# Values of the first attention jobs loaded into the accumulator, and four first-layer tiles accumulated ahead, two to a PSUM bank

## The chip, the cores and the metric

The kernel runs on one core of a Trainium2 chip. The metric is device microseconds (us) of one execution; lower is better. A core has a matmul engine (PE, with its weight loads shown as PEld), a vector engine (DVE), a scalar engine (ACT), a general engine (POOL) and a queue engine (SP) from which this kernel issues all its transfers (DMAs). Each engine works through its own list of instructions in a fixed order and waits at the first one whose inputs are not ready.

## The reference

Inputs are q, k, v of 2 batches x 8 heads x 576 positions x 64, and the weights of two feed-forward layers. For every batch and head two attentions are added: one of q, k, v averaged over groups of 4 positions (each output row is repeated 4 times), and one local attention in which a position sees only positions less than 4 away:

```
q_d, k_d, v_d = means over groups of 4 positions
out_up    = repeat(softmax(q_d k_d^T / 8) v_d, 4)
out_local = softmax(where(|i - j| < 4, q k^T / 8, -1e9)) v
x = (out_up + out_local) as 1152 tokens x 512
h = x @ w_in (512 x 2048);  x = (h * sigmoid(h)) @ w_out (2048 x 512)
out = sum over 4 experts e of p[e] * (relu(x @ w1[e]) @ w2[e])      (512 x 1024 x 512)
```

Everything is 32-bit floating point; the large products are made of three matmuls each, from a rounded value and its rest (h and l: h*h, h*l, l*h).

## The kernel before, in words

**Attention.** The work is cut into 16 jobs: 2 batches x 2 ranges of positions (256 and 320, c = 0 and 1) x 4 pairs of heads. Jobs 0 to 3 are the first range of the first batch. For a job of the first range SP loads one tile with k and q (`load_kq`, L244, 419 KB), the values in groups of four for the averaged attention (`load_vg`, L257, 288 KB) and the values in windows for the local one (`load_vw`, L250, 144 KB). A job of the second range has its own kq (323 KB) and vw tiles (L252) and reuses the averaged values of its pair of heads. The tile `vg` has one buffer, which the tail queries `qt` (L262, the last 64 positions of a batch) use too; `vw` and each kind of `kq` have two buffers. POOL folds `vg` into the averaged values `vd` (L265), and from job 4 on also q and k of a job into their averages (`qbd`, `kd`). Jobs 0 to 3 do the latter on PE and DVE (`pool_kq_first`, L292, L300).

A job then goes: scores on PE (L328, L334), maximum and subtraction on DVE (L341, L342), exponential on ACT (L346); averaged scores on PE (L352), their maximum on DVE (L366, L367) and exponential on ACT (L368); sums and division on DVE (L349 to L377) and ACT (L378); transposes on PE (L388, L390), copied by ACT (L391, L398); products with the values on PE (L416, L420); the sum of both attentions (L423, L425), and its split into `xh` (ACT, L432) and `xl` (DVE, L433). The output bank of L416 and L420 has one buffer, so a job's values wait for the split of the job before.

**First feed-forward layer.** Its weights come as 32 pieces of 512 KB (units 0 to 7 of four pieces each) through three staging buffers (L164). A piece is decoded on ACT (L189, L190), DVE (L191, L195), ACT (L197) and POOL (L198). The decoding of unit 1 is put behind job 2's `xl` on DVE, that of units 2 and 3 behind job 3's. The next load waits for a staging buffer. `g1_step` makes one 128-wide tile of h for a chunk of tokens (12 matmuls, L495), `g1_evac` turns it into g on ACT (L514 tanh, L520) and DVE (L515, L521). `g2_step` makes the second product and adds it up in `acc`, a tile of 128 x 4608 floats that is first written there. For the first chunk (256 tokens, jobs 0 to 3) the first `HOLD` = 3 tiles of h are accumulated ahead: as soon as job hp is split, `start_mm(hp)` adds its 3 matmuls to each of them. The tiles of h and g2 share three PSUM banks (`mm`); the three held tiles take them all, one bank each.

**Order.** Every step gets a priority (`at_tick`, `prio`): a load of job 1's `vg`, for example, has -26, the third weight piece -27, the kq of jobs 4 and 5 -21 and -18. A scheduler that simulates a timeline puts each engine's list in order by readiness in its simulation and then by priority. `follow` and `after` add an order edge between two instructions without a semaphore wait. The lists are made once, before the run.

**Experts** (from about 300 us on): PE products (L495, L699) with DVE, ACT and POOL work beside them; outputs are stored at the end.

Of the kernel before, what the change touches and what calls it, by code (L numbers as in the profile page):

```python
# [9 lines left out]
F32 = mybir.dt.float32  # L10
# [11 lines left out]
HP = NH // 2  # L22
# [18 lines left out]

SPLIT_AT = (-14, -11, -8, -6, -4, -4, -4, -4, -1, -1)
LOAD_AT = (-27, -13, -10)
HOLD = 3
LEAD_LOAD = 23
LEAD_SPLIT = 8
LEAD_ATTN = 11
# [14 lines left out]
def attention_moe_kernel(ctx, tc, kqa, kqb, qtl, va, vb, w64, w1d, w2d, dpr, out):  # L62
    nc = tc.nc
    PE, ACT, DVE, POOL, SP = nc.tensor, nc.scalar, nc.vector, nc.gpsimd, nc.sync
# [25 lines left out]
    acc = const.tile([128, 9 * 512], F32, name="acc")  # L90
# [31 lines left out]
    def follow(i, earlier, reason):  # L122
        tc.add_manual_dep(i.ins, earlier.ins.name, mybir.DependencyInfo(mybir.DependencyClass.NoSync, mybir.DependencyReason.DATA),
                          reason=reason)
# [81 lines left out]
    ac = actx.enter_context(tc.tile_pool(name="ac", bufs=1))  # L206
# [29 lines left out]
        pass  # L236

    kd, vd, atd = {}, {}, {}
    qt_t = {}

    def load_kq(j):
        kw = S + 6 if j.c == 0 else CT[1] + 6
        j.kq = a2.tile([128, kw + j.n], F32, tag=f"kq{j.c}", name="kq")
        SP.dma_start(out=j.kq, in_=(kqa, kqb)[j.c][j.b, j.hp])  # L244
        j.k, j.q = j.kq[:, :kw], j.kq[:, kw:]

    def load_vw(j):
        j.vw = a2.tile([72, 640], F32, tag="vw", name="vw")
        if j.c == 0:
            SP.dma_start(out=j.vw[:, 0:512], in_=va[j.b, j.hp, :, 1024:1536])  # L250
        else:
            SP.dma_start(out=j.vw, in_=vb[j.b, j.hp])  # L252

    def load_vg(j):
        if j.c == 0:
            j.vg = ac.tile([128, 256, 4], F32, tag="vg", name="vg")[0:72]
            SP.dma_start(out=j.vg, in_=va[j.b, j.hp, :, 0:1024])  # L257

    def load_tail(l):
        t = ac.tile([128, 256, 4], F32, tag="vg", name="qt")  # L260
        l.t = t[:, 0:64]
        SP.dma_start(out=l.t, in_=qtl[l.b].rearrange('p (n r) -> p n r', r=4))  # L262

    def padd(o, a, b):
        POOL.tensor_tensor(out=o, in0=a, in1=b, op=ALU.add)  # L265
# [51 lines left out]
    def after(i, earlier):  # L317
        follow(i, earlier, "PSUM bank")
# [125 lines left out]
    def plan_jobs():  # L444
        k = 0
        for b in range(NB):
            for c in range(2):
                for hp in range(HP):
                    j = Job()
                    j.i = k  # L450
                    j.b, j.c, j.hp, j.n, j.nb = b, c, hp, CT[c], CB[c]
                    t = FIRST + PER * k
                    if k > 1:
                        at_tick(t - 4, 9, load_kq, j)
                    else:
                        at_tick(FIRST - 9, k, load_kq, j)
                    at_tick(t, 9, load_vg, j)
                    at_tick(t + 1, 9, load_vw, j)
                    at_tick(t, 5, local_scores, j)
                    at_tick(t, 6, local_max, j)  # L460
                    at_tick(t, 7, pool_kq if k > 3 else pool_kq_first, j)
                    at_tick(t + 1, 4, local_exp, j)
                    at_tick(t + 2, 4, down_scores, j)
                    at_tick(t + 2, 5, down_max, j)
                    at_tick(t + 2, 6, local_sum, j)
                    at_tick(t + 3, 3, norm, j)
                    at_tick(t + 3, 8, pool_v, j)
                    at_tick(t + 5, 2, trans, j)
                    at_tick(t + 6, 1, values, j)
                    at_tick(t + 7, 0, split_x, j)  # L470
                    k += 1
            l = Job()
            l.b, l.nb = b, 0
            t = FIRST + PER * (8 * b + 4)
            at_tick(t, 9, load_tail, l)
            at_tick(t + 2, 8, tail_pool, l)
            at_tick(t + 4, 5, tail_scores, l)
# [15 lines left out]
    def mm3(ps, pairs, first, last):  # L493
        n = len(pairs)
        ins = [PE.matmul(out=ps, lhsT=l, rhs=r, start=(first and i == 0), stop=(last and i == n - 1))  # L495
               for i, (l, r) in enumerate(pairs)]
        return ins[0], ins[-1]

    def g1_pairs(u0, ft, k, c):
        wh, wl = unit[u0 + ft // 4]  # L500
        s = slice(k * 512 + (ft % 4) * 128, k * 512 + (ft % 4) * 128 + 128)
        return [(wh[:, s], xh[:, k, c]), (wh[:, s], xl[:, k, c]), (wl[:, s], xh[:, k, c])]
# [8 lines left out]
    def g1_evac(ps, ft, n):  # L511
        th = tmp_p[0].tile([128, tmp_p[1]], F32, tag="th", name="th")
        gf = tmp_p[0].tile([128, tmp_p[1]], F32, tag="gf", name="gf")
        ACT.activation(out=th[:, 0:n], in_=ps[:, 0:n], func=ACTF.Tanh, scale=0.5)  # L514
        DVE.scalar_tensor_tensor(out=gf[:, 0:n], in0=th[:, 0:n], scalar=1.0, in1=ps[:, 0:n],  # L515
                                 op0=ALU.add, op1=ALU.mult)
        flush()

        def fin():
            latest[ACT] = ACT.activation(out=gh[ft][:, 0:n], in_=gf[:, 0:n], func=ACTF.Copy)  # L520
            latest[DVE] = DVE.tensor_tensor(out=gl[ft][:, 0:n], in0=gf[:, 0:n], in1=gh[ft][:, 0:n].bitcast(F32), op=ALU.subtract)  # L521

        pend.append(fin)

    def mm_tile():
        return mm_p.tile([128, 512], F32, tag="mm", name="mm")
# [239 lines left out]
    hold = []  # L766

    def start_mm(hp):
        for i in range(HOLD):
            if hp == 0:  # L770
                hold.append(mm_tile())
            mm3(hold[i][:, 0:256], g1_pairs(0, i, hp, slice(0, 256)), hp == 0, hp == HP - 1)

    main_parts.append(start_mm)
    plan_jobs()
    for hp in range(HP):
        at_tick(FIRST + PER * hp + 8, 9, start_mm, hp)
# [31 lines left out]
    def next_step(n=1):  # L809
        prio(step[0])  # L810
        step[0] += n

    for hf in range(2):
        u0 = 4 * hf
        dt = 48 / (12 * len(CHUNKS[hf]))
        for ci, (o, n) in enumerate(CHUNKS[hf]):
            lastc = ci == len(CHUNKS[hf]) - 1
            for ft in range(8):
                next_step(dt)
                if hf == 0 and ci == 0 and ft < HOLD:  # L820
                    g1_evac(hold[ft], ft, 256)
# [138 lines left out]
```

## Time and profile before

| | |
|---|---|
| times of 3 runs | 689.97, 691.39, 691.98 us, median 691.39 us |
| profiled execution | span 693.6 us; no other time of it was recorded |
| PE busy | 659.5 us, 95% of the span |
| PEld busy | 641.9 us, 93% |
| DVE busy | 440.3 us, 63% |
| ACT busy | 332.0 us, 48% |
| POOL busy | 247.5 us, 36% |
| mean granted PE clock | 0.974 |

The span runs from the first to the last instruction of the profiled execution. "Busy" is an average over stages with different limits, so the stage of a change has to be looked at by itself. The granted clock is 1.00 at 2.4 GHz and 0.50 at 1.2 GHz.

### The profile page before, as it was taken

The page shows a single profiled execution, that of the slowest core. Times are in us where ns is not written, and L with a number is a line of the kernel's source. Part 1 is how long each engine was busy: PE and PEld are TensorE (multiplying, and loading weights), DVE is VectorE, ACT ScalarE, POOL GpSimd, SP SyncE. Part 2 cuts the span into 40 slices and gives each one's busy share as a digit, 9 for nine tenths or more (in the row PEclk, how much of TensorE's full clock was granted, in tenths as well). Part 3 has the DMA queues.
Part 4 walks back from the last instruction along what each step waited for, and adds up shares of the span by engine and source line. Part 5 has one row for each costly group of instructions (what it writes and reads, how often), then busy time and mean ns, then how long its engine had stood idle before and what let it go on. Part 6 is the DMA issues. An engine that isn't in the chain of part 4 may idle for free.

```text
span 693.6 us, 13797 instructions
## 1 busy us (share of the span) xinstructions
PE 659.5 (95%) x5516; PEld 641.9 (93%) x5516; DVE 440.3 (63%) x882; ACT 332.0 (48%) x753; POOL 247.5 (36%) x346
## 2 busy tenths in 40 slices
PE   4779779999999999999999999999999999999996
PEld 3659669999999999999999999999999999999996
DVE  4678967638664643675665985548855669756444
ACT  4559766647653532544335643345533356433321
POOL 4344762114240000344264432456232654322210
PEclk9597989999999999999999999999999999999999
DMA  8665663105250210042001420004300010000001
GB/s 248 215 183 166 184 176 96 34 1 161 92 174 1 81 44 1 1 144 70 1 1 48 136 61 1 1 2 122 93 31 1 1 60 3 1 32 17 17 31 45
DMA packets 16927, 48.16 MB, mean 69 GB/s; under 512 B 2976, under 2 KB 4256, under 8 KB 16864
## 3 DMA queue, kind: packets, MB, share of 16 engines
q1 hardware_dynamic: 16864, 47.29, 22.0%
q8 instruction: 43, 0.70, 0.4%
q14 instruction: 20, 0.16, 0.1%
HBM read 44.93 MB, written 2.36 MB: 68 GB/s over the span
## 4 chain that ended last, share of the span: by engine, by line
PE 83%; DMA 6%; DVE 6%; ACT 2%; issue 2%; POOL 1%; SPq 0%; ACTq 0%; DVEq 0%; POOLq 0%
PE mm L495 53%; PE p L699 26%; DMA stg<-in_w_dram 3%; DMA vg<-in_va_dram 2%; DVE dec L191 1%; DVE dec L195 1%; DVE gl L521 1%; PE s L328 1%; PE o L420 1%; PE t L388 1%; PE o L416 1%; DVE acc L727 1%; DVE gf L515 0%; POOL vg L265 0%; PE s L352 0%
## 5 line engine op out<-in xcount | busy, mean ns | idle before, releaser
L495 PE MATMUL mm<-xh,wbuf 128*128 128x256 f32 (+2 forms) x1280 | 268.7, 296 | 3.4 <-ACT xh L432 2.6
L495 PEld LDWEIGHTS mm<-xh,wbuf 128*128 128x128 f32 x1280 | 211.0, 190 | 4.7 <-ACT xh L432 3.0
L495 PE MATMUL mm<-xl,wbuf 128*128 128x256 f32 (+2 forms) x640 | 189.8, 297 | 0.0
L681 POOL TENSOR_TENSOR r<-r 128x128 f32<-128x128 f32 x160 | 93.5, 597 | 183.2 <-ACT r L675 143.7
L684 DVE TENSOR_TENSOR h<-r,h 128x384 fp32r<-128x384 f32 (+1 forms) x128 | 91.4, 717 | 64.6 <-ACT h L683 64.4
L495 PEld LDWEIGHTS mm<-xl,wbuf 128*128 128x128 f32 x640 | 121.6, 190 | 0.1
L683 ACT ACTIVATE h<-r 128x384 fp32r<-128x384 f32 (+1 forms) x128 | 73.2, 577 | 85.3 <-POOL r L681 54.1
L495 PE MATMUL mm<-gh,wbuf 128*128 128x256 f32 (+2 forms) x512 | 106.0, 300 | 6.4 <-ACT wbuf L197 3.5
L699 PE MATMUL p<-wext,h 128*128 128x256 f32 x672 | 91.5, 279 | 0.0
L495 PEld LDWEIGHTS mm<-gh,wbuf 128*128 128x128 f32 x512 | 83.8, 191 | 8.0 <-ACT wbuf L197 3.7
L699 PE MATMUL p<-wbuf,h 128*128 128x256 f32 x672 | 84.5, 278 | 0.0
L699 PEld LDWEIGHTS p<-wext,h 128*128 128x128 f32 x672 | 84.4, 188 | 0.0
L699 PEld LDWEIGHTS p<-wbuf,h 128*128 128x128 f32 x672 | 81.2, 188 | 0.0
L495 PE MATMUL mm<-gl,wbuf 128*128 128x256 f32 (+2 forms) x256 | 74.7, 296 | 0.5 <-DVE gl L521 0.5
L675 ACT ACTIVATE r<-mm 128x512 f32<-128x512 f32 x48 | 28.7, 597 | 75.5 <-PE mm L495 75.1
L681 DVE TENSOR_TENSOR r<-r 128x128 f32<-128x128 f32 x96 | 33.5, 349 | 37.7 <-ACT r L675 33.0
L495 PEld LDWEIGHTS mm<-gl,wbuf 128*128 128x128 f32 x256 | 48.6, 190 | 0.8 <-DVE gl L521 0.8
L521 DVE TENSOR_TENSOR gl<-gf,gh 128x256 fp32r<-128x256 f32 (+2 forms) x64 | 34.8, 547 | 18.0 <-ACT gh L520 15.4
L198 POOL TENSOR_TENSOR wbuf<-dec,wbuf 128x512 fp32r<-128x512 f32 x24 | 32.5, 1360 | 31.1 <-ACT wbuf L197 20.2
L727 DVE SCALAR_TENSOR_TENSOR acc<-p,pr,acc 128x256 f32<-128x256 f32 (+1 forms) x63 | 36.1, 605 | 5.9 <-PE p L699 5.9
L626 POOL TENSOR_TENSOR wext<-kst,wext 128x512 fp32r<-128x512 f32 x8 | 10.7, 1344 | 78.4 <-ACT wext L624 42.9
L515 DVE SCALAR_TENSOR_TENSOR gf<-th,mm 128x256 f32<-128x256 f32 (+2 forms) x64 | 28.4, 449 | 15.3 <-ACT th L514 13.6
(122 smaller groups left out, 980.2 us busy)
## 6 DMA issues: line engine op xcount, KB each, us to landing
stg<-in_w_dram SPq DMA_DIRECT2D x32, 512.0 KB, 4.3
kst<-in_w2d_dram SPq DMA_DIRECT2D x16, 512.0 KB, 3.6
kst<-in_w1d_dram SPq DMA_DIRECT2D x12, 512.0 KB, 3.6
kq<-in_kqa_dram SPq DMA_DIRECT2D x8, 419.0 KB, 3.3
kq<-in_kqb_dram SPq DMA_DIRECT2D x8, 323.0 KB, 10.8
vg<-in_va_dram SPq DMA_DIRECT2D x8, 288.0 KB
stg<-in_w1d_dram SPq DMA_DIRECT2D x4, 512.0 KB
vw<-in_vb_dram SPq DMA_DIRECT2D x8, 180.0 KB
```

The lines of the kernel that those rows point to most:

```text
L191: i = DVE.scalar_tensor_tensor(out=ai, in0=ai, scalar=3, in1=v[:, :, 0], op0=ALU.logical_shift_left, op1=ALU.bitwise_or)
L198: POOL.tensor_tensor(out=l[:, c], in0=a, in1=h[:, c].bitcast(F32), op=ALU.subtract)
L495: ins = [PE.matmul(out=ps, lhsT=l, rhs=r, start=(first and i == 0), stop=(last and i == n - 1)) for i, (l, r) in enumerate(pairs)]
L515: DVE.scalar_tensor_tensor(out=gf[:, 0:n], in0=th[:, 0:n], scalar=1.0, in1=ps[:, 0:n], op0=ALU.add, op1=ALU.mult)
L521: latest[DVE] = DVE.tensor_tensor(out=gl[ft][:, 0:n], in0=gf[:, 0:n], in1=gh[ft][:, 0:n].bitcast(F32), op=ALU.subtract)
L626: b = eng.tensor_tensor(out=l[:, r], in0=x, in1=h[:, r].bitcast(F32), op=ALU.subtract)
L675: ACT.activation(out=r[:, 0:4].rearrange("p s t -> p (s t)"), in_=ps[:, 0:512], func=ACTF.Relu)
L681: latest[eng] = eng.tensor_tensor(out=r[:, o], in0=r[:, a], in1=r[:, b], op=op)
L683: ACT.activation(out=h, in_=r[:, part], func=ACTF.Copy)
L684: latest[DVE] = DVE.tensor_tensor(out=l, in0=r[:, part], in1=h.bitcast(F32), op=ALU.subtract)
L699: ins = [PE.matmul(out=ps, lhsT=x, rhs=y, start=(opens and k == 0 and i == 0), stop=(k == 3 and i == n - 1), skip_group_check=True) for i, ...
L727: DVE.scalar_tensor_tensor(out=o, in0=ps, scalar=p, in1=o, op0=ALU.mult, op1=ALU.add)
```

## The change

The loads of the averaged values of jobs 1, 2 and 3 go to columns 0 to 3071 of `acc`, and the windowed values of jobs 2 and 3 to columns 3072 to 4095, on 72 partitions; these places have no earlier user. Job 0 and the jobs of the second batch keep the tile `vg`. The loads of the kq of jobs 4 and 5 and of the first batch's tail queries are ordered on SP behind the load of job 3's kq. `HOLD` is 4: tiles 0 and 1 share one PSUM bank, 2 and 3 another. Only the first matmul of a bank has the start flag, and the other tile's first matmul is ordered behind it.

```diff
-HOLD = 3
+HOLD = 4
...
-    qt_t = {}
+    early = []
 
     def load_kq(j):
...
-        SP.dma_start(out=j.kq, in_=(kqa, kqb)[j.c][j.b, j.hp])
+        i = SP.dma_start(out=j.kq, in_=(kqa, kqb)[j.c][j.b, j.hp])
+        if j.i == 3:
+            early.append(i)
+        elif j.i in (4, 5):
+            follow(i, early[0], "first jobs")
...
     def load_vw(j):
+        if j.i in (2, 3):
+            o = 512 * j.i + 2048
+            j.vw = acc[0:72, o:o + 512]
+            SP.dma_start(out=j.vw, in_=va[j.b, j.hp, :, 1024:1536])
+            return
...
     def load_vg(j):
         if j.c == 0:
-            j.vg = ac.tile([128, 256, 4], F32, tag="vg", name="vg")[0:72]
+            if j.i in (1, 2, 3):
+                o = 1024 * (j.i - 1)
+                j.vg = acc[0:72, o:o + 1024].rearrange("p (n r) -> p n r", r=4)
+            else:
+                j.vg = ac.tile([128, 256, 4], F32, tag="vg", name="vg")[0:72]
             SP.dma_start(out=j.vg, in_=va[j.b, j.hp, :, 0:1024])
 
     def load_tail(l):
...
-        SP.dma_start(out=l.t, in_=qtl[l.b].rearrange('p (n r) -> p n r', r=4))
+        i = SP.dma_start(out=l.t, in_=qtl[l.b].rearrange('p (n r) -> p n r', r=4))
+        if l.b == 0:
+            follow(i, early[0], "first jobs")
...
     def start_mm(hp):
         for i in range(HOLD):
-            if hp == 0:
-                hold.append(mm_tile())
-            mm3(hold[i][:, 0:256], g1_pairs(0, i, hp, slice(0, 256)), hp == 0, hp == HP - 1)
+            if hp == 0 and i % 2 == 0:
+                t = mm_tile()
+                hold.extend([t[:, 0:256], t[:, 256:512]])
+            pairs = g1_pairs(0, i, hp, slice(0, 256))
+            for m, (l, r) in enumerate(pairs):
+                opens = hp == 0 and m == 0
+                p = PE.matmul(out=hold[i], lhsT=l, rhs=r, start=opens and i % 2 == 0,
+                              stop=(hp == HP - 1 and m == len(pairs) - 1), skip_group_check=True)
+                if opens and i % 2 == 0:
+                    opened = p
+                elif opens:
+                    after(p, opened)
```

## Rows read from the trace of the kernel before

**Rows 1.** Busy time by stretch: start:end, length, each engine's busy us (instructions), clock, DMA.
```profile
0.00:100.00 100.00, 73.92 (x718) 61.77 (x719) 70.37 (x164) 62.13 (x157) 52.04 (x79) 0.83 0.66 197
100.00:686.00 586.00, 584.65 (x4794) 579.37 (x4793) 365.31 (x710) 269.90 (x596) 195.46 (x268) 1.00 0.15 47
...
24.00:44.00 20.00, 18.90 (x192) 15.49 (x192) 9.78 (x29) 10.23 (x29) 9.18 (x16) 0.78 0.47 142
44.00:82.00 38.00, 29.58 (x312) 26.23 (x311) 35.52 (x77) 28.86 (x76) 20.57 (x24) 0.87 0.59 179
50.00:60.00 10.00, 8.70 (x58) 7.61 (x59) 8.92 (x23) 8.63 (x24) 4.57 (x6) 0.50 0.66 218
```

**Rows 2.** Chain that ended last, 14 to 62 us: start, us, what.
```profile
14.86 9.41 DMA vg<-in_va_dram
...
56.77 4.24 PE mm L495 x23
```

**Rows 3.** PE in order of time, 24 to 57 us; in brackets idle time before and its releaser.
```profile
24.64 1.04 PE L388 MATMUL t<-ident,sm 128*70 128x128 f32 x4 [1.20 <-DVE sm L377]
...
42.69 0.51 PE L352 MATMUL s<-kd,qbd 128*128 128x144 f32 x2 [0.28 <-POOL qbd L265]
...
46.02 0.28 PE L495 MATMUL mm<-xl,wbuf 128*128 128x256 f32 x1
46.13 0.28 PE L495 MATMUL mm<-xh,wbuf 128*128 128x256 f32 x1
...
49.34 0.64 PE L495 MATMUL mm<-xh,wbuf 128*128 128x256 f32 x3 [2.44 <-ACT xh L432]
...
56.83 0.41 PE L495 MATMUL mm<-xl,wbuf 128*128 128x256 f32 x1
57.04 0.63 PE L495 MATMUL mm<-xh,wbuf 128*128 128x256 f32 x2
```

**Rows 4.** DVE in order of time, 44 to 63 us.
```profile
44.26 0.41 DVE L433 TENSOR_TENSOR xl<-o,xh 128x256 fp32r<-128x256 f32 x1
...
46.65 1.70 DVE L195 SCALAR_TENSOR_TENSOR dec<-stg,dec 128x512 int32<-128x512 int32 x2
48.27 0.42 DVE L425 TENSOR_TENSOR o<-o,od 128x256 f32<-128x256 f32 x1
...
62.72 0.53 DVE L341 TENSOR_REDUCE st<-s 128x5 f32<-128x350 f32 x1 [1.35 <-PE s L334]
```

**Rows 5.** The evacuation of the held tiles, ACT and DVE in order of time.
```profile
55.55 0.66 ACT L514 ACTIVATE th<-mm 128x256 f32<-128x256 f32 x2
...
56.41 0.38 DVE L515 SCALAR_TENSOR_TENSOR gf<-th,mm 128x256 f32<-128x256 f32 x1
```

**Rows 6.** PE at 15.82 us: the averaged scores of job 0.
```profile
15.82 0.84 PE L352 MATMUL s<-kd,qbd 128*128 128x144 f32 x2 [2.79 <-ACT s L346]
```

**Rows 7.** SP's issues in order of time, 5 to 14 us.
```profile
5.51 1.27 SPq L244 DMA_DIRECT2D kq<-in_kqb_dram  x2
...
11.25 1.93 SPq L164 DMA_DIRECT2D stg<-in_w_dram  x1
```

**Rows 8.** DMA issues by line: count, KB each, median us from issue to landing.
```profile
kq<-in_kqb_dram SPq DMA_DIRECT2D x8, 323.0 KB, 10.8
vg<-in_va_dram SPq DMA_DIRECT2D x8, 288.0 KB
...
vw<-in_va_dram SPq DMA_DIRECT2D x8, 144.0 KB
```

**Rows 9.** ACT in order of time, 19 to 27 us.
```profile
19.12 0.66 ACT L189 ACTIVATE dec<-stg 128x512 f32<-128x512 f32 x1 [1.40 <-DMA stg<-in_w_dram]
...
20.75 0.36 ACT L368 ACTIVATE ed<-s,st 128x144 f32<-128x144 f32 x1
...
26.70 0.67 ACT L189 ACTIVATE dec<-stg 128x512 f32<-128x512 f32 x1 [1.76 <-POOL wbuf L198]
```

**Rows 10.** Busy time by stretch, 10 to 20 us: the last two columns are DMA share and GB/s.
```profile
10.00:20.00 10.00, 4.46 (x14) 2.93 (x12) 6.53 (x19) 5.70 (x14) 4.62 (x4) 0.78 1.03 294
```

## The prediction

> **What bounds the kernel now.** I read the table of busy time by stretch first [rows 1]. From 100 to 686 us PE is busy 584.65 of 586 us at full clock: there the kernel is bound by PE, and what the change touches is over, so this stretch only moves as a block. The last 8 us are output. All that can be won or lost lies in the first 100 us, where PE is busy 73.92 us at a mean clock of 0.83. That stage has two halves. From 24 to 44 us PE is busy 18.90 of 20 us, at a clock of 0.78; from 44 to 82 us it is DVE that is full, 35.52 of 38 us, with PE idle for 8.4 us.
>
> Next, the chain of waits [rows 2]. It runs from 14.86 to 42.69 us through the single buffer of `vg`: job 1's values (9.41 us to land), the fold on POOL, then in the same way job 2's and job 3's, the tail queries, and POOL's average of job 4's queries, which releases L352 on PE at 42.69. A chain shows what came last, not by how much. PE's own list in order of time tells that [rows 3]: L352 had waited 0.28 us for POOL. PE's only idle times over 1 us from 24 to 50 us are 1.20 us at 24.64 (for job 1's division on DVE) and 2.44 us before 49.34 (for job 3's `xh`).
>
> Third, DVE from 44 us on [rows 4]: job 2's `xl` at 44.26 lets unit 1's decoding start right behind it, and two decoding steps of it (1.70 us at 46.65) stand ahead of job 3's sum at 48.27, for which PE's 2.44 us are spent. So the time at which jobs 2 and 3 end sets both the last held matmuls and the weight stream.
>
> **The change part by part.**
>
> *Fourth held tile.* Tile 3's 12 matmuls now run between 56.45 and about 60 us, in the stretch at clock 0.50, 0.21 us apart [rows 1, 3]: 12 x 0.21 = 2.5 us. They are part of the 4.24 us that the chain shows on PE [rows 2]. When they leave, the scores behind them come earlier, and DVE, which waited 1.35 us for those scores at 62.72 [rows 4], is next late: of the 2.5 us at most about 1.35 reach it. Bounds: 0 and -2.5; I take -1.35, the wait that the row shows.
>
> *The same 12 matmuls put earlier*, three in each of four passes. At full clock two are 0.11 to 0.12 us apart (46.02 and 46.13 [rows 3]). Those of jobs 2 and 3 fall beside the 2.44 us of PE idle time and cost nothing unless that idle time goes (then 6 x 0.12 = 0.7 us at full clock and 6 x 0.21 = 1.3 us at the lower one). Those of jobs 0 and 1 stand where PE is full: 6 x 0.12 = +0.7 us, bounds +0.7 and +1.3; I take +0.7, by the row nearest to these passes in time.
>
> *Values in the accumulator.* The loads of jobs 1 to 3 no longer wait for a fold, and the tail queries wait for one fold only. In the present order that ends a wait of 0.28 us [rows 3]: -0.3, the lower bound of the gain being 0. What is late next is PE itself. The lists are made anew, however, and in them the values of jobs 1 to 3 can stand earlier. The price of that is not in the trace. Its bounds: no gain if PE stays as full as it is from 24 to 44 us [rows 1], a loss as in the second rival, or the whole of job 3's wait, 2.44 us [rows 3]. I take -2.4: what PE waits for there is the end of the jobs whose loads are freed, and the job's steps (ACT, DVE) have room, with DVE busy 9.78 and ACT 10.23 of 20 us from 24 to 44 [rows 1].
>
> *Places in `acc`.* The columns are read by POOL and PE up to job 3's values, and first written by the second product's evacuation, which needs the held tiles of all four jobs first; no wait, 0.
>
> *The kq of jobs 4 and 5 later.* Their two issues stood at 5.51 us [rows 7], more than 30 us before PE's first use of them; behind job 3's kq they still land before it. The queue positions matter, though; see the second rival.
>
> *Two tiles in a bank.* Bank-wise waits are in this trace: L352 writes columns 352 and up of a bank, and waits 2.79 us for ACT's exponential of columns 0 to 279 of the same bank [rows 6]. So the two evacuations of a shared bank will take turns. Now two tanh take 0.66 us beside the DVE steps, and the second tile is done at 56.79, 1.24 us after the start [rows 5]. In turn it is about 2 x (0.33 + 0.38) = 1.42 us: 0.2 us more, under scores that PE makes meanwhile. I cost it at 0; uncovered it is +0.2 for each of two banks. In return the third bank is free, so the next tile starts without an evacuation. The Trainium skill ("PSUM — Partial Sum Buffer", section "PSUM bank collisions raise a hardware error") says that two engines must not touch one bank and the same quadrant at once, even in different columns, and that software must order them by bank. The trace agrees (the 2.79 us wait); by this rule alone the sum would be at most 0.4 us higher.
>
> *Sum:* -1.35 + 0.7 - 0.3 - 2.4 = -3.35 us. It is made against the profiled execution, whose span is 693.6 us, 2.2 us (0.3%) above the median of 691.39; I move the difference to the median: 691.39 - 3.35 = **688.0 us**.
>
> **The rivals.**
>
> *1. It goes off the path.* DVE is full from 44 to 82 us [rows 1], with a fixed amount of decoding and evacuation. If the jobs end when they did, because PE at its lower clock is the limit from 24 to 44 us, then only the 0.3 us and part of the 1.35 us remain, against the 0.7 us: -0.3 to +0.5 us, 691.2 us. For it: only 0.28 us of the long `vg` chain is a wait that PE paid. Against: PE idles 8.4 us from 44 to 82 us, so some of it is waiting for the jobs.
>
> *2. Slower: the values go ahead of unit 0's last piece.* SP issues whatever is free by priority; the kq of jobs 4 and 5 went at 5.51 us only because nothing ahead of them was free, and the last piece of unit 0 had to wait for its buffer until 11.25 [rows 7]. In the changed kernel all values of jobs 1 to 3 are free at that time: 3 x 288 + 3 x 144 = 1296 KB stand ahead of that piece in place of one 144 KB and two 323 KB loads (790 KB) [rows 8], 506 KB or 0.52 MB more. The piece issued at 11.25 is taken up at 19.12, behind the two kq issued before it; the DMA share from 10 to 20 us is 1.03, and at 294 GB/s [rows 10] the piece lands 1.8 us later. ACT waits for it already (1.40 us at 19.12), and job 1's exponential stands behind it at 20.75 [rows 9], at the end of which PE waits 1.20 us at 24.64 [rows 3]. If ACT's list keeps that order, and PE stays full behind it, +1.8 us reach job 3; with the early matmuls at the lower clock (+1.3) and the 0.3 won back: +2.8 us, 694.2 us. It decides from the point at which more than about 1 us of the delay reaches the transposes of job 1. Against it: the order on ACT is made anew, and ACT idles 1.76 us before 26.70 [rows 9], in which some of the delay can go. The Trainium skill ("DMA: Bandwidth & Descriptors", section "Queues, rings and completion order") states that each DMA engine takes its descriptors in ring order; the 7.9 us from issue to use agree, and by this rule the 1.8 us are lost for the piece in either case, which is this rival's condition.
>
> *3. Much faster.* If job 2's `xl` comes earlier than 44.26 by what DVE has free from 24 to 44 us, the weight stream starts earlier too, and the DVE-bound half moves as a whole. The stretch from 24 to 44 us at full clock would take 20 x 0.78 = 15.6 us, 4.4 us less; with the 1.35 us: -5.8 us, 685.6 us. For it: unit 1's decoding on DVE waits for that `xl`. Against: the clock and the order in which PE works would both have to change.
>
> **How the numbers follow.** My forecast (own range 686.5 to 690) has 0.38, rival 1 0.22, rival 2 0.24, rival 3 0.16. A measurement of this kernel tells about 0.3%, 2.1 us, from no change, so faster begins below 689.3 and slower above 693.5. About 0.04 of my forecast lies above 689.3. Faster: 0.34 + 0.16 = 0.50; same: 0.22 + 0.04, and 0.03 of rival 2, which a little less of a delay would bring within the bound: 0.29; slower: 0.21. The range that leaves out 2 in 10, at the far ends of rivals 2 and 3: 684.8 to 694.3 us.
>
> **What would show it.** In the profile of the changed kernel: five loads of values on SP before the load of unit 0's last piece; no load of `vg` or `qt` on the chain between 15 and 42 us; PE's wait before the last held pass under 1 us instead of 2.44; job 2's `xl` ahead of 44.26 by 1 us or more; 12 matmuls in each pass of the first-layer tiles while attention runs; PE full from 97 us or earlier, not 100. Wrong: the piece that ACT takes up at 19.12 comes after 20.5 us and job 1's transposes after 26 us (rival 2); or `xl` of job 2 stays within 0.5 us of 44.26 (rival 1). A difference that appears after 100 us would go against all of it.

## The result, and the profile after

The changed kernel takes 694.22 us (median of 20 runs, 690.44 to 698.66), the kernel before in the same comparison 689.97 us (20 runs, 686.51 to 694.18): ratio 1.0065, interval 1.0049 to 1.0081. It is 4.3 us slower, where 688.0 was forecast.

A single execution of either kernel lies up to some 4 us from its median in these 20 runs. The profiled one of the changed kernel has span 693.6 and time 695.6 us; by the same 2.0 us the profiled one of before (span 693.6) took about 695.6, more than any of its 20 runs. So I read two profiles of each kernel: run e4 is the kernel before once more (span 688.7), e14 the changed kernel once more (span 690.4). Verdicts come from times alone.

Busy time by stretch in the changed kernel, as [rows 1]: start:end, length, each engine's busy us (instructions), clock, DMA share, GB/s.

```profile
0.00:100.00 100.00, 73.85 (x701) 61.22 (x703) 71.09 (x162) 60.99 (x156) 52.45 (x77) 0.93 0.65 197
100.00:686.00 586.00, 583.37 (x4811) 577.58 (x4812) 365.56 (x713) 269.62 (x598) 194.63 (x270) 1.00 0.15 47
24.00:44.00 20.00, 19.61 (x179) 16.55 (x180) 9.63 (x28) 9.96 (x29) 4.27 (x8) 1.00 0.49 149
44.00:82.00 38.00, 28.96 (x307) 23.91 (x303) 32.48 (x77) 28.51 (x76) 19.11 (x22) 0.91 0.57 175
```

The clock of 1.00 from 24 to 44 us is not a gain over the 0.78 of [rows 1]: in that stretch of the changed kernel matmuls of 256 columns start at 34.27 and 34.48, the 0.21 us apart of the lower clock, so the record of the clock is not whole there. From 44 to 82 us DVE has gone from 35.52 busy us to 32.48, and PE has not gained by it. The start is as announced. SP issues the five loads of values ahead of unit 0's last piece, which goes at 12.25 instead of 11.25 [rows 7]:

```profile
4.04 0.40 SPq L270 DMA_DIRECT2D acc<-in_va_dram  x1
...
10.06 0.30 SPq L255 DMA_DIRECT2D acc<-in_va_dram  x1
...
12.25 1.60 SPq L164 DMA_DIRECT2D stg<-in_w_dram  x1
```

ACT takes that piece up at 20.85, 1.73 us later than in [rows 9]:

```profile
20.85 0.67 ACT L189 ACTIVATE dec<-stg 128x512 f32<-128x512 f32 x1 [0.17 <-POOL wbuf L198]
```

On the chain of waits (start, us, what) the loads of `vg` and `qt` of [rows 2] are gone between 15 and 42 us; a load of values (`vw`) and then the load of the expert shares (`pr`) lead up to 19.5 us, and behind that the chain runs over DVE and PE:

```profile
3.19 7.57 DMA vw<-in_va_dram
10.77 8.76 DMA pr<-in_dpr_dram
```

PE in order of time (start, us, instruction, in brackets idle time before it and its releaser), changed kernel:

```profile
21.30 1.07 PE L403 MATMUL t<-ident,sm 128*70 128x128 f32 x4 [4.73 <-DVE sm L392]
...
24.06 1.06 PE L403 MATMUL t<-ident,sm 128*70 128x128 f32 x4
...
47.78 0.39 PE L510 MATMUL mm<-xh,wbuf 128*128 128x256 f32 x1 [0.21 <-ACT wbuf L197]
...
49.65 0.40 PE L791 MATMUL mm<-xh,wbuf 128*128 128x256 f32 x2
50.21 0.39 PE L791 MATMUL mm<-xl,wbuf 128*128 128x256 f32 x1 [0.16 <-DVE xl L448]
...
66.50 0.28 PE L510 MATMUL mm<-gh,wbuf 128*128 128x256 f32 x1
```

and the kernel before, second profile:

```profile
48.95 1.01 PE L495 MATMUL mm<-xh,wbuf 128*128 128x256 f32 x3 [2.46 <-ACT xh L432]
...
68.07 0.28 PE L495 MATMUL mm<-gh,wbuf 128*128 128x256 f32 x1
```

The wait before the last held pass is 0.16 us instead of 2.46 (2.44 in [rows 3]). But PE does not come to that pass sooner: its first matmul starts at 49.65, against 48.95 in e4 (47.80 in e14). In the changed kernel PE first makes matmuls of the next first-layer tile (L510, from 47.78, with waits of 0.21 and 0.54 us), and the end of job 3, its `xh` on ACT, is no earlier. The changed kernel, then e4:

```profile
48.97 0.37 ACT L447 ACTIVATE xh<-o 128x256 fp32r<-128x256 f32 x1
```

```profile
48.53 0.37 ACT L432 ACTIVATE xh<-o 128x256 fp32r<-128x256 f32 x1
```

(In e14 it starts at 47.12.) The second product starts at 66.50 instead of 68.07 (64.74 in e14). So the changed kernel is ahead at 66 us. What follows is the loss. Two stretches, and a later one for comparison: first the kernel before (e4), then the changed kernel, then the changed kernel again (e14, one stretch).

```profile
75.00:90.00 15.00, 11.60 (x146) 9.87 (x144) 12.02 (x30) 10.69 (x28) 12.23 (x16) 0.98 0.75 223
90.00:105.00 15.00, 14.81 (x191) 13.29 (x191) 10.61 (x27) 10.68 (x30) 11.61 (x18) 1.00 0.61 183
236.00:266.00 30.00, 30.00 (x257) 30.00 (x256) 13.81 (x32) 10.24 (x26) 1.29 (x1) 1.00 0.11 34
```

```profile
75.00:90.00 15.00, 12.42 (x136) 10.43 (x136) 9.68 (x16) 9.86 (x25) 11.72 (x17) 0.78 0.49 144
90.00:105.00 15.00, 11.90 (x114) 10.35 (x114) 11.97 (x27) 8.98 (x23) 9.01 (x12) 0.77 0.67 209
236.00:266.00 30.00, 30.00 (x267) 30.00 (x266) 17.58 (x39) 14.72 (x34) 1.29 (x1) 1.00 0.22 70
```

```profile
90.00:105.00 15.00, 12.75 (x121) 11.08 (x121) 10.88 (x24) 8.81 (x23) 9.70 (x15) 0.77 0.60 190
```

From 90 to 105 us the kernel before issues 191 matmuls at full clock with PE full in e4; the changed one 114 and 121, at a mean clock of 0.77. The execution behind [rows 1] is no better than the changed kernel there:

```profile
90.00:105.00 15.00, 11.95 (x119) 10.79 (x120) 9.83 (x21) 9.90 (x25) 10.62 (x15) 0.77 0.55 166
```

PE's lists show one difference: every row of L334 or L349 is the mask that ends a job's scores (jobs 8 to 11). Before (e4):

```profile
74.23 0.42 PE L334 MATMUL s<-mask,ident 128*128 128x280 bf16 x1
80.30 0.29 PE L334 MATMUL s<-mask,ident 128*128 128x280 bf16 x1
88.28 0.29 PE L334 MATMUL s<-mask,ident 128*128 128x280 bf16 x1
90.02 0.39 PE L495 MATMUL mm<-gh,wbuf 128*128 128x256 f32 x1 [1.45 <-ACT wbuf L197]
94.39 0.29 PE L334 MATMUL s<-mask,ident 128*128 128x280 bf16 x1
```

Changed:

```profile
75.78 1.23 PE L510 MATMUL mm<-gh,wbuf 128*128 128x256 f32 x4 [3.08 <-POOL wbuf L198]
81.38 0.41 PE L349 MATMUL s<-mask,ident 128*128 128x280 bf16 x1
82.72 0.29 PE L349 MATMUL s<-mask,ident 128*128 128x280 bf16 x1
91.25 0.38 PE L510 MATMUL mm<-gh,wbuf 128*128 128x256 f32 x1 [2.18 <-ACT wbuf L197]
95.33 0.58 PE L510 MATMUL mm<-gh,wbuf 128*128 128x256 f32 x1 [1.65 <-ACT wbuf L197]
98.84 0.29 PE L349 MATMUL s<-mask,ident 128*128 128x280 bf16 x1
```

Before, the jobs come 6 to 8 us apart and fill the time in which PE would wait for weight pieces. In the changed kernel's list jobs 8 and 9 stand together, the next comes 16 us later, and between them PE waits for pieces, after which the clock is low for some us. e14 has the same shape (scores at 79.27, 81.38 and 97.12, waits of 1.56 and 2.04 us at 89.47 and 93.55). The execution behind [rows 1] had a wait there too (3.53 us before 93.05, for ACT's piece), without the pairing: the old list can fall into it, and in the new one both profiles show it. So these rows tell where time goes in these executions; that the new list is the cause is for the runs e9 to e11 to show.

The last job's `xl` marks the end of attention. In e4, in the changed kernel and in e9 (the change in the old order, below):

```profile
145.56 0.49 DVE L433 TENSOR_TENSOR xl<-o,xh 128x320 fp32r<-128x320 f32 x1 [0.50 <-ACT xh L432]
```

```profile
152.41 0.49 DVE L448 TENSOR_TENSOR xl<-o,xh 128x320 fp32r<-128x320 f32 x1 [0.50 <-ACT xh L447]
```

```profile
143.74 0.49 DVE L455 TENSOR_TENSOR xl<-o,xh 128x320 fp32r<-128x320 f32 x1 [0.51 <-ACT xh L454]
```

It starts at 150.66 in e14 and at 151.25 in the first profile of before. From there to the end of its span the changed kernel takes 541.2 us (e14 539.7), the kernel before 543.1 in e4 and 542.3 in its first profile. So in these profiles the loss is made while attention runs, and none of it after.

### The profile page after: what moved, and what is told of

It is laid out like the page before. It is cut to its first block, busy times and chain, and to the rows that moved or that the text cites. A ratio compares the mean times of both kernels' runs of the same rounds, so it can differ in the third digit from the quotient of the medians.

```text
span 693.6 us, 13784 instructions
## 1 busy us (share of the span) xinstructions
PE 658.2 (95%) x5516; PEld 639.5 (92%) x5516; DVE 441.3 (64%) x882; ACT 330.6 (48%) x753; POOL 247.1 (36%) x346
## 4 chain that ended last, share of the span: by engine, by line
PE 80%; DMA 6%; DVE 5%; ACT 3%; issue 3%; POOL 2%; SPq 0%; ACTq 0%; POOLq 0%; DVEq 0%
PE mm L510 48%; PE p L714 26%; DMA stg<-in_w_dram 3%; POOL wbuf L198 2%; DVE dec L191 1%; PE s L343 1%; DMA pr<-in_dpr_dram 1%; DVE dec L195 1%; PE t L403 1%; DMA vg<-in_va_dram 1%; DMA vw<-in_va_dram 1%; ACT dec L189 1%; PE o L435 1%; PE s L307 1%; PE mm L791 1%
## 5 line engine op out<-in xcount | busy, mean ns | idle before, releaser
L510 PE MATMUL mm<-xh,wbuf 128*128 128x256 f32 (+2 forms) x1248 | 260.4, 295 | 3.3 <-DVE gf L530 1.5
L510 PEld LDWEIGHTS mm<-xh,wbuf 128*128 128x128 f32 x1248 | 204.1, 188 | 5.1 <-DVE gf L530 2.6
L510 PE MATMUL mm<-xl,wbuf 128*128 128x256 f32 (+2 forms) x624 | 183.7, 294 | 0.0
L510 PEld LDWEIGHTS mm<-xl,wbuf 128*128 128x128 f32 x624 | 117.3, 188 | 0.0
L510 PE MATMUL mm<-gh,wbuf 128*128 128x256 f32 (+2 forms) x512 | 106.3, 300 | 8.5 <-ACT wbuf L197 3.8
L510 PEld LDWEIGHTS mm<-gh,wbuf 128*128 128x128 f32 x512 | 83.9, 191 | 10.8 <-ACT wbuf L197 4.3
L510 PE MATMUL mm<-gl,wbuf 128*128 128x256 f32 (+2 forms) x256 | 75.0, 298 | 0.2 <-DVE gl L536 0.2
L510 PEld LDWEIGHTS mm<-gl,wbuf 128*128 128x128 f32 x256 | 48.9, 191 | 0.6 <-DVE gl L536 0.5
L536 DVE TENSOR_TENSOR gl<-gf,gh 128x256 fp32r<-128x256 f32 (+2 forms) x64 | 33.4, 524 | 19.3 <-ACT gh L535 18.6
```

## Experiments

Each run is timed against the kernel before on the same chip (median 688.8 to 690.4 us). The expectations say TensorE, VectorE, ScalarE and GpSimd for PE, DVE, ACT and POOL. An edit moves the instruction lists, which are made once: in the changed kernel 56 of 346 instructions on POOL, 37 of 120 on SP, 217 of 882 on DVE and 183 of 735 on ACT stand at another place than before.

**e1 and e2: one half of the change each.** e1 has the loads into `acc` and the order edges, e2 the four tiles.

```diff
-HOLD = 4
+HOLD = 3
```
(e1, with `start_mm` as before; e2 keeps `start_mm` and `HOLD = 4` and has `load_kq`, `load_vw`, `load_vg` and `load_tail` as before)

> Only the value loads into the accumulator and the order edges; three held tiles in three banks, as before. Theory A (the loads' places in the queues cost the time: the small load of the expert shares lands at 19.6 us behind five loads of values, and job 0's division waits for it on DVE): this part alone has all of the loss, 3 to 6 us slower than the kernel before, about 694 us. Theory B (the fourth held tile costs it, since PE runs out of weights and falls to its lower clock): within 1.5 us of before, about 690 us.

> Only the fourth held tile, two to a bank; all loads as before. Theory A: the same as before or 1 to 2 us faster (688 to 690 us), since 12 matmuls leave the stretch after job 3. Theory B: 3 to 5 us slower, 693 to 695 us, with PE waits for weights of more than 2 us at 70 to 80 us.

e1: 692.86 us, ratio 1.0046 (1.0016 to 1.0076). e2: 696.25 us, 1.0092 (1.0056 to 1.0127). Each half is slower alone, which neither theory A nor B foresaw; that the whole is less slow than the second half is not shown, since its interval (1.0049 to 1.0081) overlaps e2's. In e2 SP has put job 7's kq, which waits for a buffer, ahead of a weight piece; SP, ACT and PE:

```profile
48.98 0.35 SPq L244 DMA_DIRECT2D kq<-in_kqb_dram  x1
...
49.86 8.29 SPq L164 DMA_DIRECT2D stg<-in_w_dram  x4
```

```profile
54.46 0.65 ACT L190 ACTIVATE stg<-stg 128x512 int32<-128x512 uint16 x1 [3.41 <-DMA stg<-in_w_dram]
```

```profile
56.98 0.83 PE L328 MATMUL s<-kq 64*64 64x70 f32 x20 [3.46 <-ACT ed L368]
```

**e3: the shares' load earlier, e4: the kernel before again.**

```diff
-    at_tick(-1, 9, lambda: SP.dma_start(out=pr, in_=dpr))
+    at_tick(FIRST - 9, 3, lambda: SP.dma_start(out=pr, in_=dpr))
```

> The changed kernel, with the small load of the expert shares (18 KB) issued between the first two kq loads in place of behind the values. Theory A in its narrow form (job 0's division waits on DVE for that load): the 4.7 us wait of PE at 21 us falls under 3 us and 1.5 to 3 us of the 4.3 us come back, 691 to 693 us. Rival (front is limited by the weights and PE at its lower clock, not by that wait): 693.5 to 695 us, as the changed kernel.

> The kernel before once more, for a second profile and for the spread. Theory P (PE's pacing: steady streams run at 113 or at 118 ns per 256-column matmul, by stretches, and differ from run to run): the stretch from 206 to 274 us, at 118 ns in the first profile of before, runs at 113 ns in part or whole in this one, with the same instruction order. Otherwise 118 ns again. Time within 0.3% of before either way.

e3: 694.65 us, 1.0080 (1.0051 to 1.0109): PE's 4.73 us before job 0's transposes fell only to 3.83, and the place of the shares' load is not the loss. e4: 690.91 us, 1.0011 (0.9980 to 1.0041), the size of no change; PE's pace from 206 to 266 us is 118 ns again, so theory P did not show here (the last section returns to it).

**e5 to e8: single waits.** In the changed kernel POOL waits 5.49 us for job 9's values, with a weight piece and job 8's keys behind it:

```profile
73.45 1.03 POOL L280 TENSOR_TENSOR vg<-vg 72x512 f32<-72x512 f32 x1 [5.49 <-DMA vg<-in_va_dram]
```

e5 (and e8, on the kernel before) gives job 9 a buffer:

```diff
+            elif j.i == 9:
+                j.vg = ac.tile([128, 256, 4], F32, tag="vg9", name="vg")[0:72]
...
+            if j.i == 9:
+                follow(i, raw[7], "buffer of its own")
```

e6 has two edges on POOL, e7 one on SP in e2's kernel:

```diff
+            if j.i == 9:
+                follow(b, pooled[8], "keys first")
+            elif j.i == 10:
+                follow(a, pooled[9], "keys first")
```
```diff
+        if j.i == 7:
+            follow(i, raw[7], "weights first")
```

> The changed kernel, with a values buffer of its own for job 9, whose load is ordered behind the eighth weight piece's. Theory C, convoy on GpSimd: the loss comes from GpSimd's in-order wait of 5.49 us for job 9's values (73.45), behind which a weight piece (TensorE waits 3.08 us before 75.78) and job 8's keys (scores at 80.3, before 73.6) stand. Then the wait is under 1 us, TensorE's wait before 75.78 under 1 us, job 8's scores by 77, and the time is 690 to 691.5. Rival R, remade order: every edit makes the compiler's instruction order anew, the loss is not tied to this one wait, and another wait of 2 to 4 us stands between 70 and 105; the time stays 693 to 696.

> The changed kernel, with two order edges on GpSimd alone, as the kernel before has it: the second step of job 9's values behind job 8's keys, and job 10's values behind job 9's keys. The wait of 5.49 us for job 9's values stays. Theory C, in the form that the keys' place in the queue behind the values is what costs: job 8's scores by 78 instead of 80.3, job 8's xl by 102 instead of 104, time 691.5 to 693. If the wait alone is what costs (weights behind it), 693.5 to 695 with TensorE's 3.08 us before 75.78 still there. Rival R: 693 to 696 and a new wait elsewhere.

> The kernel before with four held tiles, two to a bank, and no other part of the change, and the load of job 7's keys ordered behind the eighth weight piece's load. Theory H, head of the sync queue: four held tiles alone lost time because the load of that piece (49.86) stood behind job 7's keys, which waited for job 5's buffer; the piece was taken up at 54.46 and TensorE idled 3.46 us at 56.98. Then the piece is taken up by 52, TensorE's wait before 57 is under 1 us, and the time is 689.5 to 691.5. Rival (the four tiles themselves cost, by their bank or their longer hold on PSUM): 695 to 697 still.

> The kernel before, with a values buffer of its own for job 9 as in e5. It has the same wait on GpSimd (4.05 to 4.64 us before 72). Theory C: there VectorE was full in 70 to 80 and covered it, so the time is 689.5 to 691, the same as before. If the wait was paid for before too: 687 to 689. Rival R: any value from 688 to 695, with another order of the pieces.

e5: 691.82 us, 1.0041 (1.0009 to 1.0074); job 9's values were folded at 50.42, PE's 3.08 us became 1.10 (before 75.34), and POOL's list, made anew, had a wait of 2.27 us for job 10's values before 73.03. In time e5 lies between the ranges of theories C and R. e6: 692.78 us, 1.0030 (1.0002 to 1.0058), inside theory C's range for the keys, with job 8's scores at 74.83. Both may have won back a third to a half of the loss; their intervals overlap the change's. e7: 695.11 us, 1.0065 (1.0040 to 1.0090): its piece came in time, and a new wait stood elsewhere:

```profile
90.66 0.58 PE L499 MATMUL mm<-gh,wbuf 128*128 128x256 f32 x1 [3.91 <-ACT wbuf L199]
```

e8: 697.94 us, 1.0117 (1.0077 to 1.0156): one more buffer makes the kernel before 8 us slower. No single wait answered for the whole loss, new waits came in place of old ones, and an edit meant to help (e8) lost at least as much as the change; that fits rival R's mechanism, though e5 and e6 came out under its range of times.

**e9 to e11: the old order.** The decisive test: the change as it stands, but with order edges (no waits) that chain all instructions that the kernel before starts between 45 and 135 us (e10: 30 to 135) on SP, POOL, DVE and ACT in its order. From 45 us on the four lists are those of the kernel before, place by place, and PE's, which was left free, is the same as before from 77 us on (by operation, tiles and shape).

```diff
+    for ids in ORDER:
+        for a, b in zip(ids, ids[1:]):
+            tc.add_manual_dep(nc.get_inst_by_name(f"I-{b}"), f"I-{a}",
+                              mybir.DependencyInfo(mybir.DependencyClass.NoSync, mybir.DependencyReason.DATA),
+                              reason="order of before")
```

> The whole change, but with order edges that give SP, GpSimd, VectorE and ScalarE, for what the kernel before starts from 45 to 135 us, exactly the order that they have in the kernel before; TensorE's order is left to the compiler. Theory O, remade order: the change itself (the loads, the fourth tile) is worth what its first 66 us show, about 2.4 us, and the loss comes from the new order of the instructions between 50 and 105 us. Then 686.5 to 689.5, at or below before, and the half clock between 75 and 84 us and between 90 and 99 us is gone or shorter. Rival P, the change itself costs: 692.5 to 696, as it stands.

> Four held tiles, two to a bank, alone (no early values), with the order of SP, GpSimd, VectorE and ScalarE up to 135 us exactly as in the kernel before, so that only TensorE's list differs. Theory O: the fourth tile costs nothing by itself, 688 to 691. Rival P (the twelve more matmuls in each of four passes, or two tiles in a bank, hold up the jobs): 694 to 697, like e2 and e7.

> The early values alone (three held tiles in three banks), with the order of the four engines from 45 to 135 us as in the kernel before. Theory O: 688 to 690.5, below e1's 692.9. Rival P (the early loads hold up the first pieces and the shares): 692 to 694, like e1.

| | lists as made | with the old order |
|---|---|---|
| whole change | 1.0065 (1.0049 to 1.0081) | e9: 690.62 us, 0.9996 (0.9970 to 1.0022) |
| four tiles | e2: 1.0092 (1.0056 to 1.0127) | e10: 691.38 us, 1.0018 (0.9993 to 1.0042) |
| values | e1: 1.0046 (1.0016 to 1.0076) | e11: 691.14 us, 1.0003 (0.9974 to 1.0033) |

Three times the loss goes with the new order, which is theory O against rival P: 1.0065 against 0.9996 is 0.7%, 4.8 us. For the whole change and for the four tiles the intervals lie apart; for the values they overlap (1.0016 to 1.0033), so there it is likely and not shown. All three times lie above theory O's ranges by 0.4 to 1.1 us and below rival P's. The other half of O failed: e9 is not faster than before, 686.5 to 689.5 was expected. e9's stretches and PE's list, from the fastest of its 12 executions (687.36 us):

```profile
75.00:90.00 15.00, 11.81 (x169) 10.02 (x168) 12.76 (x28) 11.16 (x30) 13.38 (x16) 1.00 0.69 209
90.00:105.00 15.00, 14.85 (x177) 13.51 (x174) 10.76 (x28) 11.09 (x32) 10.81 (x19) 1.00 0.55 163
```

```profile
73.36 0.29 PE L356 MATMUL s<-mask,ident 128*128 128x280 bf16 x1
78.90 0.29 PE L356 MATMUL s<-mask,ident 128*128 128x280 bf16 x1
87.29 0.29 PE L356 MATMUL s<-mask,ident 128*128 128x280 bf16 x1
92.61 0.29 PE L356 MATMUL s<-mask,ident 128*128 128x280 bf16 x1
```

In this execution the even spacing of the jobs, the full clock and the short waits (at most 1.01 us from 80 to 105) are back, and the jobs come 0.9 to 1.8 us earlier than in e4, whose profiled execution (690.87) lies at its median.

**e12 to e16: which list, and what takes up the gain.** e12 chains SP and POOL alone, e15 ACT alone, e16 DVE alone (against e9, with the rows of `ORDER` as SP, POOL, DVE, ACT, `ORDER[:2]`, `ORDER[3:]` and `ORDER[2:3]`); e13 is e9 with e5's buffer, its load four places earlier on SP; e14 is the change again.

```diff
-    (622, 541, 550, 559, 568, 1345, 668, 1472, 677, 751, 1143, 740,
+    (622, 541, 550, 559, 568, 1345, 1143, 668, 1472, 677, 751, 740,
```
(e13: the load of job 9's values, instruction 1143, in SP's chain)

> The whole change, with the order of the kernel before (45 to 135 us) given to SP and GpSimd alone; VectorE and ScalarE are ordered by the compiler. Theory Q, the loss is in the in-order queues of SP and GpSimd (values before keys, weight pieces behind a load): 689 to 691.5, as e9. Rival V, it is the order on VectorE and ScalarE (splits of weights and gelu steps ahead of the jobs' softmax): 692.5 to 695, like the change as it stands, and ScalarE's waits between 85 and 95 us remain.

> e9 (the whole change, four engines in the old order from 45 to 135 us) with a values buffer of its own for job 9, whose load stands four places earlier in SP's list (about 57 us). Theory C, GpSimd's wait of 4 to 5 us before 72 is what takes up the gain of the start: the wait falls under 1 us and the time is 687 to 689, below both kernels. Rival: VectorE is full from 60 to 80 us in that order and the wait is covered, 689.5 to 691.5 as e9.

> The changed kernel once more, unedited, beside e12 and e13: 693 to 695.5, and a profile with GpSimd's wait of about 5 us for job 9's values and TensorE's half clock between 75 and 100 us, if these belong to its order and not to one execution.

> The whole change with the old order (45 to 135 us) given to ScalarE alone; the compiler then comes back to nearly the old order on the other engines by itself. Theory S, ScalarE's list, in which weight pieces and the jobs' exponentials are interleaved, carries the loss: 689.5 to 691.5, as e9. Rival V2, it is VectorE's: 692.5 to 695.

> The whole change with the old order (45 to 135 us) given to VectorE alone; ScalarE, GpSimd and SP keep a new order in places. Theory S: 692.5 to 695, like the change as it stands, with TensorE's waits for ScalarE's weight pieces between 75 and 100 us. Rival V2: 689.5 to 691.5, and those waits are gone.

e12: 694.03 us, 1.0064 (1.0034 to 1.0094), no better than the change, so the lists of SP and POOL do not carry the loss and theory Q falls; e12 also has the keys where e6 put them, which speaks against theory C. e14: 694.59 us, 1.0076 (1.0048 to 1.0104). e15: 692.59 us, 1.0042 (1.0017 to 1.0067). e16: 692.45 us, 1.0041 (1.0016 to 1.0066). Neither S nor V2: with either list alone about 0.4% of loss stays, although in e15 little but some 30 instructions of DVE still stood at other places. A wait of PE in e12, in e15 and in e16:

```profile
97.08 0.41 PE L410 MATMUL t<-ident,ed 128*72 128x128 f32 x2 [2.66 <-ACT ed L398]
```

```profile
88.60 0.81 PE L435 MATMUL o<-atd,vd 72*64 72x80 f32 x8 [3.92 <-DVE xl L452]
```

```profile
90.55 0.64 PE L409 MATMUL t<-ident,ed 128*72 128x128 f32 x2 [2.90 <-ACT ed L397]
```

Each has a wait of 2.7 us or more between 88 and 98, for ACT, DVE and ACT; e9 and e10 have none above 1.1 us from 80 to 105. But neither long waits nor paired jobs mark the loss in general: e2 and e8, the two slowest, have no wait above 1.8 us from 75 to 105, e8, e15 and e16 have no pair, and e6, with a pair (74.83 and 75.70, then 90.82), loses least. What goes with it is the end of attention: the last `xl` starts at 143.1 to 147.7 in e9, e10, e11 and e13 and at 147.0 in e6, but at 149.1 to 158.2 in every other run with a list made anew. Which places of the list cost this stays open.

e13: 691.22 us, 1.0004 (0.9968 to 1.0039). POOL's wait, 4.64 us in e9, is gone, as these rows of e9 and then e13 show, and the time is the same:

```profile
70.49 1.29 POOL L287 TENSOR_TENSOR vg<-vg 72x512 f32<-72x512 f32 x1 [4.64 <-DMA vg<-in_va_dram]
```

```profile
68.98 1.49 POOL L292 TENSOR_TENSOR vg<-vg 72x512 f32<-72x512 f32 x1
```

The Trainium skill ("Perfetto Trace Analysis", section "Optimization Strategy") advises to find the gaps of the engine one optimizes for and to make what they wait for start sooner. Here it led to no version faster than before: e13 removed a wait of POOL and the time stayed, and in e5, where PE's 3.08 us became 1.10, and in e7 the remade lists had new waits. No version that beats both kernels came out of these runs.

## Why the prediction was wrong

- *The step that failed is the sum: a term that it put at nothing.* It took the lists from 60 us on as given ("this stretch only moves as a block" for what follows 100 us, and only a gain for lists "made anew"). The lists behind 45 us were made anew too. Holding them in the old order from 45 to 135 us takes away 0.7% (change against e9), 4.8 us; none of the three rivals named it.
- *The values, -2.4 us:* the number came true where it was read, but not by its mechanism. PE's 2.46 us became 0.16 because PE had the next tile to work on; job 3's `xh` was at 48.97 and 47.12, against 48.92 and 48.53 before, so its end came 1.4 us earlier in e14 and not at all in the first profile. The second product started 1.6 us earlier (3.3 in e14). In the times none of it reached the end: e9 lies at -0.30 to +0.22%, -2.1 to +1.5 us, against -3.35. That is rival 1's time and not its mechanism, for in e9's profile job 2's `xl` is at 40.33, where rival 1 has 44.26. What takes the gain up is not POOL's wait (e13) and stays open.
- *The sum by its own rule:* the -2.4 takes PE's wait as gone, and for that case the prediction says that the six early matmuls of jobs 2 and 3 cost 0.7 us. The sum leaves them out; with them it is -2.65 us, 688.7.
- *The fourth tile, -1.35 and +0.7 us:* not seen. e10, which also holds the price of two tiles in a bank, is at -0.07 to +0.42%, where -0.09% was summed. The two evacuations of a bank did take turns: the first pair took 2.47 us (52.65 to 55.12; 2.46 in e14), where 1.42 was worked out.
- *Rival 2* gave 694.2 us, and 694.22 was measured: that is a coincidence. Its signs differ between executions. In the first profile the piece was taken up 1.73 us later, near the 1.8 worked out, though the last wait before it was for POOL, and job 1's transposes were at 24.06 (24.64 in [rows 3]), not after 26; in e14 the piece was at 22.80 and the transposes at 26.19. Its mechanism is not the loss; e11 has the same five early loads and is at 1.0003.
- *Rival 1's sign* differs between executions: job 2's `xl` at 43.96 in the first profile (0.3 us earlier than in [rows 4]), at 42.11 in e14.
- *After 100 us:* I held PE to be full from 97 us and any difference after 100 us to be against the forecast. The loss lies before the last `xl` (152.41), in part behind 100 us: there the changed kernel still had work left that e4 had done (PE busy 73.85 and 71.74 of the first 100 us, against 77.98). And from 236 to 266 us the changed kernel is the faster one (last section).
- *The base:* 691.39 rested on three runs; 20 runs and more gave 688.8 to 690.4. And the rows of before came from an execution slower than all 20.

## What to carry to other kernels

Where a scheduler writes the lists, compare the lists of the two kernels first and ask what the new order costs in places that the edit doesn't touch. To price an edit itself, hold the rest in the old order with order edges and time that. A wait in one profile is a place to look, not a price: take it away, and see whether the time moves.

## What the runs showed of the hardware

- PE has two steady paces at full clock. In 236 to 266 us, PE full and the clock 1.00, matmuls of 256 columns start 118 ns apart in the kernel before (257 rows touch the window, in its first profile and in e4) and in e8; in the changed kernel they start 113 ns apart (267 rows), and so they do in e1, with the values alone. The pace does not belong to the kernel: from 207 to 232 us the changed kernel runs at 118 ns in its first profile and at 113 ns in e14. What sets it was not found. The Trainium skill ("TensorE: Matmul & The Clock Gate", section "Wait — 56ns, not 53.3ns?") gives the columns at 2.4 GHz plus about 2.5 ns, which would be 109.2 ns (an estimate by that page); both paces here are longer.
- PE's granted clock falls to its lower level (0.50, 1.2 GHz) for some us in stretches with waits. In the changed kernel the mean from 75 to 90 us is 0.78, with 3.08 us without work before 75.78, and from 90 to 105 us 0.77, with 2.18 and 1.65 us before 91.25 and 95.33; in e9, whose waits from 80 to 105 us are at most 1.01 us, both are 1.00. One long wait is not needed: in e2 the mean from 90 to 105 us is 0.80, with no wait above 1.10 us from 75 to 105. Matmuls of 256 columns are 0.21 us apart at the lower level and 0.11 to 0.12 at the full one, so a wait that goes with such a fall costs more than its length.
